# Free heads' output rows behind the second layer's first scores, and a shorter wait for runs of slots

## The chip, the cores and the metric

The kernel runs on one core of a Trainium2 chip. The metric is device time in microseconds (us); the time before is the median of three runs. One execution was also taken with the hardware profiler, and all rows below come from it. PE is the matmul engine, DVE and ACT are the vector and scalar engines, POOL the general one, and SP is the queue from which nearly all loads are issued.

## The reference

Eight batch rows, one token each, go twice through the same block A and block B, with the same weights and the same caches both times.

```python
def _A_ref(x, k_cache, v_cache, wq, wo):          # caches (8, 8, 4096, 256)
    q = (x @ wq).reshape(B, Sq, Hq, Dh)           # 16 query heads, 8 KV heads
    ...
    scores = jnp.einsum("bhqd,bhkd->bhqk", q, k) * (Dh ** -0.5)
    p = _softmax(scores, axis=-1)
    o = jnp.einsum("bhqk,bhkd->bhqd", p, v)
    return o...reshape(B, Sq, Hq * Dh) @ wo       # the output projection
...
x = x + _A_ref(_layernorm(x), A_k_cache, A_v_cache, A_wq, A_wo)
x = x + _B_ref(_layernorm(x), B_w1, B_w2, B_w3, B_w4)     # an MLP
x = x + _A_ref(...)      # second layer: same K and V, new queries
x = x + _B_ref(...)
```

A batch row's second-layer queries need the row's whole first layer and its MLP, but the K and V that they meet are those of the first layer. With one token, block B's shifts along the sequence fill all four parts with zeros, so that w1 and w2 have no effect; what stays is the layer norms and gelu(layernorm @ w3) @ w4, here called the MLP.

## The kernel before, in words

**Slots.** K and V stream through 30 slots of 512 KB (`QUARTERS`); a head's K or V is four slots, and a load takes up to four slots that lie side by side. In layer 0, five of a row's eight heads (3 to 7, "kept heads") leave their K in the slots, wholly or in part, and two leave V, so that the second layer need not load it again. Heads 0 to 2 are the "free heads": they keep nothing.

**The order of the work.** While a row goes from layer 0 to layer 1 (the "crossing": `mid`, a chain of small steps, the MLP and the new queries), the next row's free heads have their V products done: `run([("b", 0, b + 1, h) for h in free_heads])`. Their scores came earlier, and their V is loaded slot by slot (`MOST = 1`). Behind the crossing the row's second layer begins (`both(1, b, order2)`): its first heads' K stands in slots already, so their scores (line 1136) need only the new query, and they are what frees these slots.

**The planner.** `Plan.schedule` runs when the kernel is built. It is a list scheduler: every step (`plan.op`) has an engine, modelled durations, dependences and a priority, the lower the sooner. Whenever an engine is free in the model, it takes the ready step of lowest priority value. Program order is the usual priority (`len(plan.ops)`); short chains behind scores get `hi`, 100,000 lower, and the MLP's chain and the free heads' V products lower values still. The result is a fixed order of instructions on each engine, with semaphores where a step needs another engine's. When PE would idle, the planner puts in filler matmuls (line 1689).

**Output rows.** `wo_row` (line 1312, in `back`) multiplies one head's result `oT` with its part of `wo` in four matmuls and adds it up in one PSUM bank, `psR`, over the first seven heads of a row. `oT` has two buffers, so a head's `oT` (written on DVE, line 1292) waits for the row step of the head before the last. The bank is also used by the crossing's statistics (line 763), and the free heads' rows stand behind them in the program.

**Loads.** SP issues loads in one fixed order. For each, `next_kv` looks for a run of `m` free slots; it may wait for one until `late`, and then takes the largest run there is, so that the load goes out in pieces:

```python
late = max(free["sp"], dma_end - self.LEAD)
...
for t in [max(free["sp"], times[0])] + [x for x in times if free["sp"] < x <= late]:
    fit = [(k, a) for k, a in runs(t) if k >= m]
    if fit: break
else:
    t = max(late, times[0])
    m = min(m, max(k for k, a in runs(t)))
```

`dma_end` is when the planner thinks that the loads issued so far will have landed. It also thinks that a load starts 4.0 us (`ISSUE`) after its issue.

Of the kernel before, what the change touches and what calls it, by code (L numbers as in the profile page):

```python
# [52 lines left out]
Q1 = 176  # L53
ROWS = True
SHORT = 0.1


class Op:
# [28 lines left out]
class Plan:  # L87
# [5 lines left out]
    HOT = 3500  # L93


    ISSUE, LEAD = 4.0, 3.5
    BLOCK, FETCH = 128, 6.0
    LAT = {"pe": 0.25, "dve": 0.06, "act": 0.06, "pool": 0.05, "sp": 0.4}

# [374 lines left out]
def bass_interleave_layers__gqa_block_cached__mixer_s_mlp__decode_kernel(  # L474
# [20 lines left out]
    plan = Plan()  # L495
# [141 lines left out]
    def issue_kv(o, n, q):  # L637
# [6 lines left out]
        o.dma = (slot_sem[q], 16 * slot_n[q])  # L644
        o.dur = ((n << 15) / 26.88e3 + 8 * 0.008) / FASTER + SHORT * (n < 3)

# [55 lines left out]
    for i in range(2):  # L702
        plan.op("dve", lambda v, i=i: v.memset(psP[i][:, 0:DH], 0.0), 0.3, "const", wr=["pz"],
                banks=[f"P{i}"])
# [531 lines left out]
    def back(layer, b, h):  # L1236
# [10 lines left out]
        hi = len(plan.ops) - 10 ** 5  # L1247
# [6 lines left out]
        for u in range(4):  # L1254
# [17 lines left out]
            if u not in keep_v:  # L1272
# [7 lines left out]
                banks=[bk], prio=hi)  # L1280

        def sum_mm(t):
# [8 lines left out]
           prio=hi)  # L1291
# [14 lines left out]
        if k <= turn_at:  # L1306
            def wo_row(t):
                last = None
                for i in range(4):
                    a = (4 * h + i) * D  # L1310
                    r = 64 * layer + 32 * (i % 2)
                    last = t.matmul(psR[r:r + 1, 0:D], oT[no][:, i % 2, i // 2:i // 2 + 1],  # L1312
                                    wo_sb[:, a:a + D], start=(k == 1 and i < 2),
                                    stop=(k == turn_at and i >= 2),
                                    skip_group_check=True, tile_position=(0, r))
                return last
            o = plan.op("pe", wo_row, (0.41, 0.78, 448, 4), "wor", rd=[("oT", no), "wo0"], wr=[kr],
                        banks=["R"], prio=hi)
            if k == HOTK and layer == 0:
                o.hot = True  # L1320
        xkeys = [ok] + (["x3all" if b < B - 2 else ("xf", b - B + 2)] if layer else [])
        if k == turn_at:
            for a, mts in [(0, range(2)), (2 * P, range(2, NC5))]:
# [7 lines left out]
                def turn(t, a=a, mts=mts):  # L1331
# [7 lines left out]
                   prio=hi, width=YW)  # L1339
# [246 lines left out]
    free_heads = list(range(HKV - KEEP_K))  # L1586
# [19 lines left out]
    def run(tasks):  # L1606
        for t in tasks:
            (fronts_of if t[0] == "f" else back)(*t[1:])
# [140 lines left out]
```

## Time and profile before

| | |
|---|---|
| median of three runs | 1085.01 us (1085.01 to 1085.93) |
| profiled execution, its own time | 1082.09 us |
| its span, first to last instruction | 1080.2 us |
| loads in it | 436.38 MB, mean 404 GB/s |
| PE busy | 943.6 us (87%) |
| DVE, ACT busy | 598.8 us, 339.3 us |
| output rows (line 1312) | 444 matmuls, 65.1 us |
| loads of four slots, of one slot | 73 + 64, 130 + 11 |

In rows that group instructions stand line, engine, operation, output and inputs, shapes, count, busy time, the mean in ns, and the idle time before. In rows of a timeline the first two numbers are start and length in us. In rows of windows the pairs are an engine's busy time and its instructions, and the last three numbers are the granted PE clock, the share of the 16 DMA engines that was busy, and GB/s. In rows of waits stand the total, the number of waits and the longest one.

### The profile page before, as it was taken

The page shows a single profiled execution, that of the slowest core. Times are in us where ns is not written, and L with a number is a line of the kernel's source. Part 1 is how long each engine was busy: PE and PEld are TensorE (multiplying, and loading weights), DVE is VectorE, ACT ScalarE, POOL GpSimd, SP SyncE. Part 2 cuts the span into 40 slices and gives each one's busy share as a digit, 9 for nine tenths or more (in the row PEclk, how much of TensorE's full clock was granted, in tenths as well). Part 3 has the DMA queues.
Part 4 walks back from the last instruction along what each step waited for, and adds up shares of the span by engine and source line. Part 5 has one row for each costly group of instructions (what it writes and reads, how often), then busy time and mean ns, then how long its engine had stood idle before and what let it go on. Part 6 is the DMA issues. An engine that isn't in the chain of part 4 may idle for free.

```text
span 1080.2 us, 33935 instructions
## 1 busy us (share of the span) xinstructions
PE 943.6 (87%) x15144; PEld 651.1 (60%) x15144; DVE 598.8 (55%) x1895; ACT 339.3 (31%) x940; POOL 97.9 (9%) x278
## 2 busy tenths in 40 slices
PE   5889798988988889898898989998889999998895
PEld 4556556665656656566566655666556675666663
DVE  3345445555665556455565555565556655565564
ACT  1235113341234403254023531334214341343150
POOL 0000000000110101011010100101001000110010
PEclk9899989998999989999899998999989997999895
DMA  9999999999999999999999999999999999999994
GB/s 356 407 428 420 392 380 424 426 397 410 388 425 425 421 404 413 424 427 418 385 409 427 423 415 388 427 425 423 402 389 426 426 407 398 399 427 418 348 422 189
DMA packets 51342, 436.38 MB, mean 404 GB/s; under 512 B 5486, under 2 KB 8700, under 8 KB 27260
## 3 DMA queue, kind: packets, MB, share of 16 engines
q1 hardware_dynamic: 51108, 433.95, 97.9%
q8 instruction: 119, 1.95, 0.7%
q10 hardware_dynamic: 88, 0.26, 0.1%
q14 instruction: 27, 0.22, 0.1%
HBM read 434.18 MB, written 0.01 MB: 402 GB/s over the span
## 4 chain that ended last, share of the span: by engine, by line
DMA 50%; PE 39%; DVE 5%; issue 2%; SPq 1%; ACT 1%; POOL 0%; POOLq 0%; DVEq 0%
DMA kv<-in_A_k_cache_dram 27%; DMA kv<-in_A_v_cache_dram 22%; PE psT L1482 14%; PE psP L1262 7%; PE psT L1378 6%; PE psM L1136 3%; PE psM L891 2%; PE psR L1312 2%; PE psM L1053 1%; SPq L626 1%; DMA w_sb<-in_B_w_dram 1%; DVE kv L1413 1%; DVE oS L1276 1%; DVE oS L1278 1%; PE psP L1286 1%
## 5 line engine op out<-in xcount | busy, mean ns | idle before, releaser
L1482 PE MATMUL psT<-ident_f,kv 128*128 128x128 f32 x2752 | 376.3, 285 | 21.6 <-DMA kv<-in_A_k_cache_dram 19.3
L1482 PEld LDWEIGHTS psT<-ident_f,kv 128*128 128x128 f32 x2752 | 305.7, 144 | 101.2 <-issue 55.2
L1413 DVE COPY kv<-psT 128x512 f32<-128x512 f32 x381 | 260.8, 690 | 180.9 <-PE psT L1482 173.3
L1414 ACT COPY kv<-psT 128x512 f32<-128x512 f32 x339 | 197.5, 586 | 389.4 <-PE psT L1482 301.1
L1262 PE MATMUL psP<-kv,pT 128*2 128x256 bf16 x4096 | 178.3, 289 | 17.9 <-DMA kv<-in_A_v_cache_dram 14.5
L1378 PE MATMUL psT<-kv,qz 128*32 128x512 bf16 x1664 | 135.9, 399 | 6.3 <-ACT kv L1414 4.0
L1262 PEld LDWEIGHTS psP<-kv,pT 128*2 128x2 bf16 x4096 | 85.0, 83 | 62.1 <-DMA kv<-in_A_v_cache_dram 27.1
L1216 POOL PARTITION_ALL_REDUCE gm<-pm x128 | 45.4, 354 | 763.1 <-DVE pm L1214 754.2
L1276 DVE CAST oS<-psP 128x256 bf16<-128x256 f32 x128 | 53.9, 421 | 65.2 <-PE psP L1262 64.5
L1226 ACT ACTIVATE pT<-sS,nb,fac 128x32 bf16<-128x32 bf16 x128 | 52.6, 417 | 115.3 <-DVE nb L1220 115.3
L1312 PE MATMUL psR<-wo_sb,oT 128*1 128x448 bf16 x444 | 65.1, 377 | 9.9 <-DVE oT L1292 3.8
L1230 POOL PARTITION_ALL_REDUCE Db<-rs x128 | 51.0, 398 | 185.7 <-ACT pT L1226 185.7
L1286 PEld LDWEIGHTS psP<-sel,oS 128*128 128x128 bf16 x512 | 23.7, 99 | 61.4 <-DVE oS L1278 57.2
L1286 PE MATMUL psP<-sel,oS 128*128 128x2 bf16 x512 | 32.1, 166 | 31.9 <-DVE oS L1278 30.3
L1378 PEld LDWEIGHTS psT<-kv,qz 128*32 128x32 bf16 x1664 | 35.3, 96 | 40.3 <-issue 12.4
L1226 ACT ACTIVATE pT<-sS,nb 128x32 bf16<-128x32 bf16 x128 | 40.8, 326 | 59.2 <-DVE nb L1220 59.2
L1689 PE MATMUL psP<-ident_f 128*128 128x256 bf16 x357 | 58.2, 286 | 0.0
L1278 DVE TENSOR_TENSOR oS<-psP,oS 128x256 bf16<-128x256 f32 x128 | 54.1, 423 | 2.9
L1393 DVE CAST sr<-psT 128x512 bf16<-128x512 f32 x51 | 35.2, 691 | 31.9 <-PE psT L1378 31.7
L1136 PEld LDWEIGHTS psM<-qz,kv 128*128 128x128 bf16 x1344 | 41.2, 99 | 18.8 <-issue 5.8
L1136 PE MATMUL psM<-qz,kv 128*128 128x48 bf16 x1344 | 47.8, 187 | 5.4 <-DVE kv L1413 3.4
L1394 ACT CAST sr<-psT 128x512 bf16<-128x512 f32 x53 | 31.0, 585 | 53.4 <-PE psT L1378 53.4
(190 smaller groups left out, 778.8 us busy)
## 6 DMA issues: line engine op xcount, KB each, us to landing
kv<-in_A_k_cache_dram SPq DMA_DIRECT2D x73, 2048.0 KB, 22.2
kv<-in_A_v_cache_dram SPq DMA_DIRECT2D x64, 2048.0 KB, 19.0
kv<-in_A_v_cache_dram SPq DMA_DIRECT2D x130, 512.0 KB, 8.5
kv<-in_A_v_cache_dram SPq DMA_DIRECT2D x14, 1536.0 KB, 9.0
kv<-in_A_k_cache_dram SPq DMA_DIRECT2D x11, 1536.0 KB, 17.3
kv<-in_A_v_cache_dram SPq DMA_DIRECT2D x14, 1024.0 KB, 7.2
kv<-in_A_k_cache_dram SPq DMA_DIRECT2D x8, 1024.0 KB, 8.0
kv<-in_A_k_cache_dram SPq DMA_DIRECT2D x11, 512.0 KB, 14.1
```

Of the source, the lines that this page charges most:

```text
L1136: last = t.matmul(ps[:, SB + 2 * i:SB + 2 * i + 2 * REP], a()[:, c:256:2], bcast(rhs(c), REP, 1), start=(c == 0), stop=(c == 1))
L1226: return a.activation(pT[nr][:, :, :].rearrange("p i j -> p j i")[:, jj, :], sview[:, jj, :], ACT.Exp, bias=nb[nm][:, jj:jj + 1], scale=sc ...
L1262: last = t.matmul(ps[g4:g4 + 2, PV0:PV0 + DH], pT[nr][:, k, :], slot_ap(q, s * 256, 256), start=(i < 4), stop=(i >= 28), skip_group_check= ...
L1276: plan.op("dve", lambda v: v.tensor_copy(oS[:, 0, :], po), 0.36, "o", rd=[("pv", par, x) for x in range(4)], wr=["oS0"], banks=[bk], prio=hi)
L1278: plan.op("dve", lambda v: v.tensor_tensor(oS[:, 1, :], po, oS[:, 0, :], ALU.subtract), 0.36, "o", rd=["oS0"] + [("pv", par, x) for x in r ...
L1286: last = t.matmul(ps[:, PV1 + 2 * c:PV1 + 2 * c + 2], oS[:, w, c:DH:2], sel[:, :], start=(w == 0), stop=(w == 1))
L1312: last = t.matmul(psR[r:r + 1, 0:D], oT[no][:, i % 2, i // 2:i // 2 + 1], wo_sb[:, a:a + D], start=(k == 1 and i < 2), stop=(k == turn_at ...
L1378: last = t.matmul(psT[bank][32 * g:32 * g + 32, :], qz[:, a:a + 32], slot_ap(qs[g // 2], g % 2 * 1024, 1024)[:, c:1024:2], start=(half == ...
L1413: return e.tensor_copy(dst, psT[bank][:, :])
L1414: return e.copy(dst, psT[bank][:, :])
L1482: last = t.transpose(psT[bank][:, s * P:(s + 1) * P], src, ident_f[:, :])
L1689: return t.matmul(dst, ident_b, bcast(ident_b[:, 0:n // 4], 4, 1), start=True, stop=True)
```

## The change

Two edits. The row steps of layer 0's free heads, from batch row 1 on, get the priority of a step 100 places further on in the program, instead of one that is 100,000 places ahead. And the planner stops waiting for a run of slots 5.0 us before the end of its loads, instead of 3.5. Nothing that is computed changes.

```diff
 SHORT = 0.1
+WOR_AFTER = 100
...
-    ISSUE, LEAD = 4.0, 3.5
+    ISSUE, LEAD = 4.0, 5.0
...
             o = plan.op("pe", wo_row, (0.41, 0.78, 448, 4), "wor", rd=[("oT", no), "wo0"], wr=[kr],
-                        banks=["R"], prio=hi)
+                        banks=["R"], prio=len(plan.ops) + WOR_AFTER if layer == 0 and b and h in free_heads else hi)
```

## The prediction

> **What bounds the kernel now.** I read the page first, for the span, the engines, the DMA rate in 40 slices and the chain that ended last.
>
> ```profile
> span 1080.2 us, 33935 instructions
> ...
> GB/s 356 407 428 420 392 380 424 426 397 410 388 425 425 421 404 413 424 427 418 385 409 427 423 415 388 427 425 423 402 389 426 426 407 398 399 427 418 348 422 189
> DMA packets 51342, 436.38 MB, mean 404 GB/s; under 512 B 5486, under 2 KB 8700, under 8 KB 27260
> ...
> DMA 50%; PE 39%; DVE 5%; issue 2%; SPq 1%; ACT 1%; POOL 0%; POOLq 0%; DVEq 0%
> ```
>
> Half of the last chain is loads, and the bytes are fixed: at the 424 to 427 GB/s of the good slices 436.38 MB would take 436.38/425 = 1027 us. The row of 40 slices (27 us each) shows where the rest goes: besides the start and the end, one or two slices dip to 380 to 415 in each stretch of some five, once per batch row. So the second view is the table by windows at those dips; behind the length stand the busy times of PE, weight loads, DVE, ACT and POOL with their counts, then the granted clock, the DMA share and GB/s. First three dips, then a stretch of single-slot loads, then one of full loads:
>
> ```profile
> 270.00:280.00 10.00, 9.91 (x227) 6.33 (x224) 5.84 (x25) 1.06 (x4) 0.35 (x1) 0.76 0.96 325
> 400.00:410.00 10.00, 9.11 (x189) 5.76 (x189) 5.56 (x25) 2.40 (x7) 0.75 (x2) 0.77 1.00 381
> 1000.00:1030.00 30.00, 27.02 (x628) 19.84 (x621) 17.87 (x84) 5.79 (x16) 1.86 (x5) 0.86 0.97 353
> 390.00:400.00 10.00, 8.77 (x226) 5.79 (x223) 5.12 (x30) 0.21 (x1) 0.00 (x0) 0.88 1.03 407
> 430.00:440.00 10.00, 8.65 (x124) 5.95 (x120) 5.06 (x14) 4.26 (x12) 0.94 (x3) 1.00 1.00 424
> ```
>
> The dips are the crossings, where a batch row goes from layer 0 through the MLP to its second-layer queries. Two things are told apart by the last two rows: small loads alone cost a little (407 against 424), and something else in the crossing takes the rate down to 325 to 381. What the loads wait for there is in the waits of the SP queue, which issues them:
>
> ```profile
> SPq L643 <- PE psP L1262: 631.4, 137, 25.6
> ...
> SPq L643 <- PE psM L1136: 69.5, 30, 7.8
> ```
>
> A load waits until its slots are free, and slots are freed by PE: by the PV products (L1262) and by scores (L1136 is the form that the first heads after a crossing use). Elsewhere these waits are harmless because loads stand far ahead; in a crossing they decide. One crossing in the order of time, PE's own lines:
>
> ```profile
> 401.30 0.96 PE L1312 MATMUL psR<-wo_sb,oT 128*1 128x448 bf16 x4
> ...
> 402.47 0.95 PE L1312 MATMUL psR<-wo_sb,oT 128*1 128x448 bf16 x4
> 403.36 0.82 PE L1136 MATMUL psM<-qz,kv 128*128 128x48 bf16 x16
> ...
> 404.61 1.38 PE L1136 MATMUL psM<-qz,kv 128*128 128x48 bf16 x48
> ...
> 406.82 0.54 PE L1312 MATMUL psR<-wo_sb,oT 128*1 128x448 bf16 x4
> 407.30 0.40 PE L1689 MATMUL psP<-ident_f 128*128 128x256 bf16 x2
> ...
> 408.14 0.84 PE L1689 MATMUL psT<-ident_f 128*128 128x512 bf16 x3
> 409.62 0.37 PE L1136 MATMUL psM<-qz,kh 128*128 128x48 bf16 x8 [0.64 <-ACT kh L1422]
> ```
>
> and, from the same stretch, the query's last step on DVE, the oT of the third free head, and the load on SP:
>
> ```profile
> 401.15 0.21 DVE L1533 SCALAR_TENSOR_TENSOR qz<-cs_q,mom,psM 128x4 bf16<-128x4 f32 x1
> ...
> 406.17 0.15 DVE L1292 TENSOR_TENSOR oT<-psP,rc 128x4 bf16<-128x4 f32 x1
> ```
>
> ```profile
> 405.62 0.81 SPq L643 DMA_DIRECT2D kv<-in_A_v_cache_dram  x2
> ```
>
> The query is there at 401.15 + 0.21 = 401.36, but two output rows (L1312) of the next batch row's free heads run first, and the scores that free three slots start at 403.36 and end at 405.99; SP issues at 405.62, on their release. Behind the scores PE is short of work: it runs filler matmuls (L1689), 0.40 and 0.84, and idles 0.64.
>
> **Part one: 21 output rows move behind the scores.** They are layer 0, batch rows 1 to 7, heads 0 to 2: 84 of the matmuls of this group of the page.
>
> ```profile
> L1312 PE MATMUL psR<-wo_sb,oT 128*1 128x448 bf16 x444 | 65.1, 377 | 9.9 <-DVE oT L1292 3.8
> ```
>
> At four matmuls a step that is 21 of 111 steps. All seven crossings by window, L1312 alone, each from about the query to the end of the first head's scores (length, L1312 busy, clock, DMA share, GB/s; five of the rows and the sum):
>
> ```profile
> 139.40:143.60 4.20, 0.91 (x4) 0.73 0.94 338
> 273.10:277.70 4.60, 1.55 (x8) 0.81 1.05 304
> ...
> 528.60:534.60 6.00, 1.91 (x8) 0.53 1.00 382
> 658.20:663.10 4.90, 1.50 (x8) 0.76 0.97 340
> ...
> 915.70:921.20 5.50, 1.91 (x8) 0.62 1.02 381
> sum 34.90, PE 11.54; mean PE 1.65
> ```
>
> So 1.65 us of rows stand in front of the end of the scores in a crossing, 11.54 in all, mostly at half the clock (0.95 for four, against 0.54 at 406.82). With the new priority (program place plus 100, where it had been minus 100,000) they lose against everything that is ready within some two heads of program behind them, so the scores end up to 1.65 us sooner and so does the issue on them. The PV products keep their place, as they are more urgent in both. The rows themselves I cost at nothing: the two that join the third behind the scores take 2 x 0.54 = 1.08 us, under the 0.40 + 0.84 + 0.64 = 1.88 us of filler and idle there. If that cover is gone they cost 1.08 us in front of the second head's scores, and what the first scores gain the second lose. A row issues no DMA and stands in no queue but PE's. What waits for it: the DVE write of the third head's oT, which reuses the first head's buffer, behind it the PV bank of that head; and much later the seventh head's copies of the row sums.
>
> What 1.65 us sooner is worth is bounded by what DMA loses there. Against the 407 of single-slot loads, a window loses length x (407 - rate)/407: 4.20 x 69/407 = 0.71 in the first, 1.16 in the second, 0.35 in the last, and 4.26 us in all seven. Behind the scores the loss goes on, while the loads that the same chain releases come late; the windows there, with the filler (L1689) as the selected line (the first, the fifth and the last of seven):
>
> ```profile
> 143.60:152.00 8.40, 1.63 (x6) 1.00 0.94 346
> ...
> 663.10:670.00 6.90, 1.34 (x6) 1.00 1.01 421
> ...
> 921.20:928.00 6.80, 1.06 (x4) 1.00 1.00 379
> ```
>
> In the same way these lose 1.26 in the first, -0.24 in the fifth, 0.47 in the last and 3.74 in all seven. The filler in them (1.63, 1.34, 1.06; the others lie between) bears out that PE has room there in every crossing. The best is then -(4.26 + 3.74) = -8.0 us. The other end is a loss: one row at 0.54 in front of something needed, in seven crossings, +3.8. I take 3.0 of the 4.26, because a loss of 0.61 in the mean is smaller than the 1.65 by which the release comes forward, but some of it lies ahead of the release and belongs to PV; and 1.0 of the 3.74, which only inherits the shift: **-4.0 us**.
>
> **Part two: LEAD from 3.5 to 5.0.** When the slots for a load of m are not free together, the planner waits for them until 3.5 us before it thinks the queue will run dry, then sends a smaller piece. Now it stops 1.5 us sooner. The order of loads on SP is the same; pieces become smaller and leave earlier. Where loads stand far ahead the limit is not reached, so this too acts in the crossings, and alone in the last one, which has no rows to move: there 30 x (407 - 353)/407 = 4.0 us are lost, the most that it could return beside part one. Its price is more small loads. At 407 GB/s a slot of 512 KB (524,288 B) takes 1.288 us and at 424 it takes 1.237, so a slot cut off costs 0.052 us. Today's pieces:
>
> ```profile
> kv<-in_A_k_cache_dram SPq DMA_DIRECT2D x73, 2048.0 KB, 22.2
> kv<-in_A_v_cache_dram SPq DMA_DIRECT2D x64, 2048.0 KB, 19.0
> kv<-in_A_v_cache_dram SPq DMA_DIRECT2D x130, 512.0 KB, 8.5
> ```
>
> Most of the 130 are cut on purpose (84 belong to the seven rows' free heads, loaded slot by slot). If 30 slots more are cut, the price is 30 x 0.052 = 1.6 us; if none, nothing. For the gain I take 1.6, some 40% of the last crossing's 4.0. Gain and price cancel: **0**, between -4.0 and the +9.4 of the second rival.
>
> **The sum** is made against the profiled execution's 1082.09 us (span 1080.2 and 1.9 around it), which is 2.9 below the median of the runs, 1085.01: 1082.1 - 4.0 = 1078.1 there, and 1085.0 - 4.0 = **1081.0 us** as a median.
>
> **Rivals.** *Nothing to win (1085).* The dips may not be late releases. For it: the DMA share at 400 to 410 is 1.00 at 381 GB/s, so the engines are counted as busy, with longer packets, not as empty. Against: the lowest rates of the crossings (304, 338, 340) stand in the windows with the rows in front. It gives within 2.2 us of no change.
>
> *Small loads (1090).* A planner that gives up sooner leaves slots scattered, and then later runs of four are missing too, in the good stretches also. 137 loads have four slots; if a third of them, 45, break into singles, that is 180 x 0.052 = 9.4 us, less the 4.0: 1085.0 + 5.4 = 1090.4. The turning point is 77 more slots loaded singly (4.0/0.052). For it: pieces are already common in crossings. Against: the two rows of four-slot loads land 19 to 22 us after issue, about four loads ahead at 2 MB / 424 GB/s = 4.9 us each, where the new limit is not reached. At the far end, if each cut-off slot came to an empty queue and cost its own 1.29 us once more, 30 of them would cost 39 us and the time would be 1120; of the 0.22 below I give this 0.02.
>
> The Trainium skill, "DMA: Bandwidth & Descriptors", section Measured, speaks against this part: it asks for transfers of at least 1 MiB, and its section on the anatomy of one DMA puts a fixed 2.0 us on each, measured on GpSimd's path. By that, 30 further loads would cost an estimated 60 us if nothing hid it. The trace does not bear it out for loads in a queue, as the loads of 388 to 404 show, an answer of the DMA view:
>
> ```profile
> DMA packets 1682, 6.44 MB, mean 402 GB/s; under 512 B 187, under 2 KB 187, under 8 KB 1610
> ...
> kv<-in_A_v_cache_dram SPq DMA_DIRECT2D x9, 512.0 KB, 7.3
> kv<-in_A_v_cache_dram SPq DMA_DIRECT2D x1, 1024.0 KB, 7.6
> ```
>
> Nine loads of one slot and one of two, issued in 16 us, go with a mean of 402 GB/s, 1.3 us a slot; the rule has 2.0 + 1.2.
>
> *The rows come too late (1089).* If the planner puts the first head's row behind the second head's scores, past 412, the third head's oT waits some 6 us (it is written at 406.17 now), its PV bank is held, and the slots of the next head on that bank come free late. If 0.54 us per crossing is lost, it is the +3.8 above: 1085.0 + 3.8 = 1088.8. Against: the filler at 407 to 409 shows free PE before that.
>
> **How the numbers follow.** 2.2 us (0.2%) is about what a measurement of this kernel can tell from no change. Forecast 0.50; nothing to win 0.20; small loads 0.22; rows too late 0.08. So faster 0.50, same 0.20, slower 0.30. The range reaches from the best of part one with the forecast's gain of part two unpaid (1085.0 - 8.0 - 1.6 = 1075.4, rounded to 1075.5) to the small loads' 1090. What is left out is the far end of the small loads and the case that all of the crossings' loss comes back with the last one's. The forecast's own range is 1076 to 1082.5.
>
> **What would show it.** Right: in the crossings L1136 comes straight behind the query's qz, with no L1312 between them; L1312 stands where L1689 stood, with fewer fillers; SP's wait on L1136 is shorter than 69.5; the seven windows' rates rise from 304 to 382 GB/s towards 407, with the slices' dips. For part two: more than 130 loads of 512 KB, by up to some 30, and the window 1000 to 1030 above 353. Wrong: rates in the crossings as before although L1136 is earlier (the first rival); over 77 more single-slot loads or good slices under 420 (the second); a new wait of DVE at L1292 for L1312 (the third).

## The result, and the profile after

| | before | after |
|---|---|---|
| median of the runs, us | 1085.47 | 1078.49 |
| ratio to before, 95% interval | | 0.9931 [0.9911, 0.9950] |
| the same, runs repeated later on one chip | 1086.97 | 1079.43, 0.9941 [0.9917, 0.9964] |
| profiled execution, its span, us | 1080.2 | 1074.4 |

The change makes the kernel 0.6 to 0.7% faster. The forecast was 4 us, the median moved by 7. The two halves of the forecast were wrong in opposite directions, as the experiments show: the moved rows give nothing, and the shorter wait, priced at nothing, gives all of it. That the time still fell into the forecast's range is luck: one error made up for part of the other. Single executions scatter (those of the kernel before from 1079 to 1093 us over all its runs), so ratios of many runs decide below and profiles tell only where.

The page after, and the waits of SP (lines stand one further down than before, from 56 on):

```profile
span 1074.4 us, 33999 instructions
...
GB/s 367 407 426 422 391 390 427 426 419 399 408 426 425 416 394 420 425 426 409 382 423 425 425 414 397 426 425 423 399 397 423 427 415 398 409 426 417 355 423 193
DMA packets 56526, 436.39 MB, mean 406 GB/s; under 512 B 6062, under 2 KB 9276, under 8 KB 34236
...
DMA 49%; PE 42%; DVE 4%; SPq 2%; issue 1%; ACT 1%; POOL 0%; DVEq 0%
```

```profile
SPq L644 <- PE psP L1263: 530.7, 139, 27.1
SPq L644 <- PE psT L1379: 195.6, 48, 18.0
SPq L644 <- PE psM L1137: 65.9, 36, 5.1
```

SP waits 100 us less for the PV products (631.4 before) and 90 more for the scores in rows (L1379, 106.6 before): the waits have changed places and not gone. The waits for the first heads' scores, which the moved rows were to shorten, are nearly as before (69.5). The good slices are as before (423 to 427), so the further small loads have not spread into them. The pieces:

```profile
kv<-in_A_k_cache_dram SPq DMA_DIRECT2D x68, 2048.0 KB, 23.2
kv<-in_A_v_cache_dram SPq DMA_DIRECT2D x61, 2048.0 KB, 17.1
kv<-in_A_v_cache_dram SPq DMA_DIRECT2D x163, 512.0 KB, 8.1
...
kv<-in_A_k_cache_dram SPq DMA_DIRECT2D x28, 512.0 KB, 9.5
```

There are 191 one-slot loads where there were 141, and 129 of four slots where there were 137. The crossings, first from the query to the end of the first head's scores with the output rows (L1313) selected, then behind it with the filler (L1690), in windows that follow the shifted times:

```profile
137.20:143.10 5.90, 0.91 (x4) 0.50 1.00 376
268.90:274.50 5.60, 0.91 (x4) 0.57 0.98 374
...
911.30:916.30 5.00, 0.00 (x2) 0.58 1.00 372
sum 35.20, PE 4.73; mean PE 0.68
```

```profile
143.10:151.50 8.40, 1.69 (x6) 0.94 0.99 353
...
659.90:666.80 6.90, 0.84 (x3) 1.00 1.02 411
...
916.30:923.10 6.80, 1.12 (x4) 1.00 1.02 405
```

Of the 11.54 us of rows in front of the scores' end 4.73 are left, but the seven windows up to it are no shorter: 35.2 us against 34.9. The loss of both sets of windows against 407 GB/s has fallen from 8.0 to 3.2 us. That isn't the whole account: in the ten us ahead of each query the rates are lower than before (372 in the mean, against 396), which gives 4.0 us back. The windows alone do not say where the time went. One crossing on PE, at the same place as in the prediction:

```profile
397.72 0.96 PE L1313 MATMUL psR<-wo_sb,oT 128*1 128x448 bf16 x4
...
399.33 1.23 PE L1137 MATMUL psM<-qz,kv 128*128 128x48 bf16 x32
...
400.81 0.57 PE L1137 MATMUL psM<-qz,kv 128*128 128x48 bf16 x16
401.67 0.39 PE L1263 MATMUL psP<-kv,pT 128*2 128x256 bf16 x8 [0.29 <-DMA kv<-in_A_v_cache_dram]
402.00 0.57 PE L1137 MATMUL psM<-qz,kv 128*128 128x48 bf16 x16
402.50 0.54 PE L1313 MATMUL psR<-wo_sb,oT 128*1 128x448 bf16 x4
```

One row still comes first; the second has moved behind the scores. In its stead PE waits 0.29 us, in the middle of the scores, for a V load of the free heads.

### The profile page after: what moved, and what is told of

Same layout as the page of the kernel before. It is cut to its first block, busy times and chain, and to the rows that moved or that the text cites. A ratio compares the mean times of both kernels' runs of the same rounds, so it can differ in the third digit from the quotient of the medians.

```text
span 1074.4 us, 33999 instructions
## 1 busy us (share of the span) xinstructions
PE 943.5 (88%) x15150; PEld 651.8 (61%) x15150; DVE 593.6 (55%) x1889; ACT 344.1 (32%) x946; POOL 97.9 (9%) x278
## 4 chain that ended last, share of the span: by engine, by line
DMA 49%; PE 42%; DVE 4%; SPq 2%; issue 1%; ACT 1%; POOL 0%; DVEq 0%
DMA kv<-in_A_k_cache_dram 30%; DMA kv<-in_A_v_cache_dram 18%; PE psT L1483 16%; PE psP L1263 8%; PE psT L1379 5%; PE psM L1137 3%; PE psR L1313 2%; SPq L627 2%; PE psM L892 1%; PE psM L1054 1%; PE psP L1690 1%; DVE kv L1414 1%; DMA w_sb<-in_B_w_dram 1%; DVE oS L1279 1%; DVE oS L1277 1%
## 5 line engine op out<-in xcount | busy, mean ns | idle before, releaser
L1414 DVE COPY kv<-psT 128x512 f32<-128x512 f32 x368 | 252.9, 691 | 189.2 <-PE psT L1483 180.1
L1415 ACT COPY kv<-psT 128x512 f32<-128x512 f32 x352 | 205.3, 587 | 384.7 <-PE psT L1483 300.6
L1379 PE MATMUL psT<-kv,qz 128*32 128x512 bf16 x1664 | 133.7, 395 | 4.7 <-ACT kv L1415 3.4
L1313 PE MATMUL psR<-wo_sb,oT 128*1 128x448 bf16 x444 | 62.4, 366 | 8.2 <-DVE oT L1293 4.0
L1379 PEld LDWEIGHTS psT<-kv,qz 128*32 128x32 bf16 x1664 | 34.6, 95 | 38.1 <-issue 12.3
L1690 PE MATMUL psP<-ident_f 128*128 128x256 bf16 x359 | 56.7, 284 | 0.0
L1394 DVE CAST sr<-psT 128x512 bf16<-128x512 f32 x55 | 38.0, 692 | 31.2 <-PE psT L1379 31.0
L1137 PEld LDWEIGHTS psM<-qz,kv 128*128 128x128 bf16 x1344 | 43.6, 102 | 18.0 <-issue 8.1
L1137 PE MATMUL psM<-qz,kv 128*128 128x48 bf16 x1344 | 50.5, 191 | 4.1 <-issue 2.2
L1395 ACT CAST sr<-psT 128x512 bf16<-128x512 f32 x49 | 28.7, 586 | 52.1 <-PE psT L1379 49.5
## 6 DMA issues: line engine op xcount, KB each, us to landing
kv<-in_A_v_cache_dram SPq DMA_DIRECT2D x7, 1536.0 KB, 11.1
```

Source lines behind the costliest of these rows:

```text
L1137: last = t.matmul(ps[:, SB + 2 * i:SB + 2 * i + 2 * REP], a()[:, c:256:2], bcast(rhs(c), REP, 1), start=(c == 0), stop=(c == 1))
L1379: last = t.matmul(psT[bank][32 * g:32 * g + 32, :], qz[:, a:a + 32], slot_ap(qs[g // 2], g % 2 * 1024, 1024)[:, c:1024:2], start=(half == ...
L1414: return e.tensor_copy(dst, psT[bank][:, :])
L1415: return e.copy(dst, psT[bank][:, :])
L1690: return t.matmul(dst, ident_b, bcast(ident_b[:, 0:n // 4], 4, 1), start=True, stop=True)
```

## The experiments

**The two halves alone, and the change again.** Theory A is the prediction's (the rows carry it), theory B that the shorter wait does, C that each needs the other. Rows alone, from the changed kernel:

```diff
-    ISSUE, LEAD = 4.0, 5.0
+    ISSUE, LEAD = 4.0, 3.5
```

> The rows alone: WOR_AFTER as in the change, LEAD back at 3.5. Theory A (the prediction's): the rows carry the gain; about 4 us faster than before, a ratio of 0.996, and one-slot loads stay near before's 130 + 11. Theory B: the shorter wait carries the gain, since in the changed kernel one row per crossing still runs before the first scores and the first head's scores end no sooner on the mean; then within 2 us of before, 0.998 to 1.002. Theory C: the two need each other; then this one is slower than before.

Measured: 1.0029 [1.0009, 1.0049], slower. The wait alone, from the kernel before:

```diff
-    ISSUE, LEAD = 4.0, 3.5
+    ISSUE, LEAD = 4.0, 5.0
```

> The shorter wait alone: LEAD 5.0, the output rows as before. Theory A: within 1.5 us of before (gain and price of smaller loads cancel), 0.9985 to 1.0015. Theory B: all or most of the gain, 4 to 7 us faster, 0.9935 to 0.996, with some 50 more one-slot loads, as in the changed kernel. Theory C: slower than before or no change.

Measured: 0.9940 [0.9920, 0.9959]. The change once more:

> The changed kernel itself once more, beside the two halves on the same chip. All theories: 0.991 to 0.995, as first measured. It gives the sum against which the halves are added, and a second profile: where its lead over before in loaded bytes comes at the same places as in the first, it belongs to the schedule; where it does not (one step of 1.6 us at 100 MB, away from a crossing), it belongs to the single execution.

Measured: 0.9941 [0.9917, 0.9964]. So B holds: the wait alone gives as much as both. A falls, and so does C, which had both halves slower or useless alone. The step at 100 MB that this expectation names is in the second profile too (between 90 and 100 loaded MB the lead over before's trace grows by 1.4 us, by 1.6 in the first). So by the expectation's own rule it belongs to the schedule, but not all of it: the traces with LEAD at 3.5 gain 0.6 to 0.7 us on before's there as well.

**The rows' place, with everything else held.** The rows alone also got another plan, so two kernels keep the plan of before. In the first, 13 rows are put behind the scores in PE's finished order (`line`; `j` is the place behind the last of these scores):

```diff
     plan.schedule()
+    for o in reversed([o for o in line if o in moved_rows]):
...
+        line.insert(j, o)
     plan.synchronise()
```

> The kernel before with its plan kept to the last slot, load and priority; in PE's finished order alone the 13 free-head rows that stood in front of the first head's scores are put straight behind them. Theory A (the prediction's step: sooner scores are sooner loads): 3 to 4 us faster, 0.996 to 0.997. Theory B (the scores' end is not what the loads in the crossing are short of, and the rows only change places): within 1 us of before, 0.999 to 1.001. Theory C (the third head's oT and with it slots come late): 2 us slower or more. If this one is not slower, then what made the rows alone slower (1.0029) was the planner's other slots and loads, not the rows' place.

Measured: 1.0016 [0.9998, 1.0033]. In the second, the rows compute one of their 448 columns and leave out the others, so that their time is all but gone:

```diff
-  last = t.matmul(psR[r:r + 1, 0:D], ..., wo_sb[:, a:a + D], ...)
+  w = 1 if layer == 0 and b and h in free_heads else D
+  last = t.matmul(psR[r:r + 1, 0:w], ..., wo_sb[:, a:a + w], ...)
```

> The kernel before with its plan kept; the 21 free-head row steps compute one of their 448 columns (the other columns of these heads are left out of the projection), so nearly all of their PE time is gone from the crossings: up to 11.5 us of it in front of the first scores' end. It is the most that moving them could ever give. Theory A (scores in time are loads in time): 4 us faster or more, 0.996 or less. Theory B (the rows' place does not matter to the loads): within 1.5 us of before, 0.9985 to 1.0015.

Measured: 0.9993 [0.9972, 1.0013]. So theory A falls here too: both intervals lie above its 0.996 to 0.997, and hold theory B's no change. Even taking nearly all of the rows' time away is worth nothing that can be measured. The first kernel's timeline shows why; this is the same crossing as in the prediction:

```profile
403.27 0.59 PE L1265 MATMUL psP<-kv,pT 128*2 128x256 bf16 x8 [0.28 <-DMA kv<-in_A_v_cache_dram]
403.79 0.82 PE L1137 MATMUL psM<-qz,kv 128*128 128x48 bf16 x16
404.54 0.60 PE L1265 MATMUL psP<-kv,pT 128*2 128x256 bf16 x8
405.07 2.10 PE L1137 MATMUL psM<-qz,kv 128*128 128x48 bf16 x48
407.10 1.47 PE L1315 MATMUL psR<-wo_sb,oT 128*1 128x448 bf16 x8
```

The last 48 of the scores as a window, first before, then in this kernel (length, L1136 or L1137 busy, clock, DMA share, GB/s):

```profile
404.61:405.99 1.38, 1.38 (x48) 1.00 0.99 365
```

```profile
405.07:407.17 2.10, 2.10 (x48) 0.50 1.00 361
```

No row stands before the scores, but PV products do, and they wait for their V to land; and the last 48 score matmuls take 2.10 us where they took 1.38. Over the seven crossings, from the query's row sums, the first score starts at 2.07 us (2.08 with the thin rows) instead of 2.58, and the first head's scores end at 5.66 (5.73) instead of 5.60. So of the 1.65 us of rows only 0.5 come out as an earlier start (in this crossing PV products and a wait for V stand in front of the scores), and the scores then take those 0.5 us back, since they run at a lower clock. From the first score to the last the granted clock is 0.80 in the mean of before's seven crossings, 0.55 with the rows moved by hand and 0.52 with the thin ones, and the 64 matmuls are busy for 2.31, 2.89 and 2.97 us. Why the clock is lower there no run shows.

**What a small load costs.**

```diff
...
-  o.emit = lambda eng: eng.dma_start(dst, src)
...
+  for i in range(n):
+      d = eng.dma_start(kv[:, (q + i) * 2048:(q + i + 1) * 2048], src[:, i * 2048:(i + 1) * 2048])
...
```

> The kernel before with its plan kept; every load of 2, 3 or 4 slots is issued as that many loads of one slot at the same moment, one behind the other. It prices small loads alone, without any earlier issue. Prediction's price: 0.052 us for a slot loaded singly; 137 x 4 + 25 x 3 + 22 x 2 = 667 slots, so 35 us slower, 1.032. By the packets' own times (159 against 614/4 = 153.5 ns for 4 KB) 667 x 8 x 5.5 ns = 29 us, 1.027. If a load had a fixed price that the queue does not hide, much more: at 1 us each over 480 further loads 480 us. If small pieces help by themselves, as each can be worked on when it lands, less than 20 us.

Measured: 1127.39 us against 1087.39, 1.0369 [1.0344, 1.0393]. 40.0 us over 667 slots are 0.060 us a slot; the prediction had 0.052.

```profile
GB/s 339 399 408 406 381 371 409 407 392 404 361 408 408 404 374 398 408 409 406 376 406 407 409 406 378 407 407 408 377 372 408 408 387 383 384 408 388 293 402 195
...
kv<-in_A_v_cache_dram SPq DMA_DIRECT2D x456, 512.0 KB, 11.4
```

The price is a lower rate everywhere, 408 in slices that had 425. A fixed price for each load can't be large: the 483 further loads cost 0.083 us each, all told.

**How long the planner should wait.** From 3.5 in both directions, with the rows as before except in the second:

> LEAD 4.25, rows as before: half of the step from 3.5 to 5.0. If what pays is that loads leave sooner (loads issued under 4 us before the one ahead of them lands: 19 in before, 4 at LEAD 5.0), about half of the gain: 2 to 4 us faster than before, 0.996 to 0.998, with one-slot loads between 141 and 203. If the gain at 5.0 is a lucky plan (another draw of slots), no order in LEAD: anywhere from 0.993 to 1.003.

Measured at 4.25: 0.9932 [0.9908, 0.9956], all of the gain and not half.

> LEAD 6.5 with the rows moved as in the change: the same step of 1.5 again. Theory A: slower than the changed kernel by the price of further pieces, 0.052 us for each slot loaded singly (30 more: 1.6 us). Theory B: if earlier issue is what pays and the rate in the crossings (352 to 410 GB/s in the five us behind the query) has room left up to 407, a further 1 to 3 us faster; if the queue stands far enough ahead at 5.0, no change or slower by the pieces.

Measured at 6.5, rows moved: 0.9950 [0.9932, 0.9968], no further gain.

> LEAD 8.0, rows as before: the planner hardly waits for runs. The late loads are gone as at 5.0, and the price of small loads goes on: some 100 one-slot loads more than before at 0.052 us are 5 us, and fewer four-slot loads. If early issue and price are the two terms: the gain of 5.0 kept and another 2 to 5 us of price, so 0.996 to 0.999. If small loads cost nothing: as at 5.0, 0.994.

Measured at 8.0: 0.9958 [0.9939, 0.9977]; 246 one-slot loads.

> LEAD 2.0, rows as before: the planner waits 1.5 us longer for runs than before. If late loads are the cost (20 issued under 4 us before the one ahead lands, which lose 11.9 us in before's trace; 6 and 4.4 us at 4.25), more of them and later ones: 5 to 20 us slower than before, 1.005 to 1.02, although it has fewer one-slot loads. If the price of small loads were what decides, faster than before.

Measured at 2.0: 1.0123 [1.0090, 1.0156], although it has the fewest one-slot loads, 126. All four plans above 3.5 are faster and the one below it is slower, so the gain isn't one lucky plan. What too long a wait does is plainest in this kernel, on SP and in windows of 1 us (POOL's busy time, the clock, the DMA share, GB/s):

```profile
542.06 1.17 SPq L643 DMA_DIRECT2D kv<-in_A_v_cache_dram  x2
```

```profile
541.00:542.00 1.00, 0.00 (x0) 1.00 0.21 74
542.00:543.00 1.00, 0.35 (x1) 1.00 0.00 0
543.00:544.00 1.00, 0.03 (x1) 1.00 1.07 188
544.00:545.00 1.00, 0.36 (x1) 1.00 0.89 319
545.00:546.00 1.00, 0.12 (x1) 1.00 1.00 426
```

```profile
SPq L643 <- PE psP L1262: 6.3, 2, 5.6
```

```profile
kv<-in_A_v_cache_dram SPq DMA_DIRECT2D x1, 1024.0 KB, 5.0
```

SP waited up to 5.6 us for PV products to free a run of two slots; the queue ran empty; and the load, issued at 542.06, moved nothing before 543 and landed after 5.0 us, where its 1 MB takes 2.5 at 424 GB/s. So this load, which came to an empty queue, lost some 2.5 us. The Trainium skill, "DMA: Bandwidth & Descriptors", section on the anatomy of one DMA, has about 2.0 us of fixed cost for a DMA that GpSimd issues; these loads are issued by SP.

Counted over whole traces, a load is called late here if it is issued less than 4 us before the load ahead of it lands; it loses what its landing lies behind that one beyond 1.228 us a slot (1.272 for a single slot), which is what most loads take that are issued well ahead. Two loads in the first 3 us of the kernel, which no LEAD touches, are left out; the expectation for LEAD 2.0 counts them, and so has 20 and 11.9 us for before, and 6 and 4.4 for 4.25.

| kernel | LEAD | ratio | late loads, us lost | one-slot loads |
|---|---|---|---|---|
| wait 2.0 | 2.0 | 1.0123 | 20, 20.6 | 126 |
| before | 3.5 | 1 | 18, 9.8 | 141 |
| rows alone | 3.5 | 1.0029 | 17, 14.2 | 145 |
| rows by hand | 3.5 | 1.0016 | 15, 13.3 | 141 |
| thin rows | 3.5 | 0.9993 | 14, 14.7 | 141 |
| wait 4.25 | 4.25 | 0.9932 | 4, 1.5 | 173 |
| wait 5.0 | 5.0 | 0.9940 | 3, 3.6 | 203 |
| the change | 5.0 | 0.9931 | 5, 4.5 | 191 |
| the change again | 5.0 | 0.9941 | 4, 2.1 | 191 |
| wait 6.5, rows moved | 6.5 | 0.9950 | 1, 0.0 | 225 |
| wait 8.0 | 8.0 | 0.9958 | 2, 1.5 | 246 |

From 3.5 to 4.25 the late loads go, and beyond it their number hardly falls any more while the price goes on: 8.0 is 0.26% (2.8 us) behind 4.25 with 73 more one-slot loads, which at 0.060 would be 4.4; the two intervals overlap.

Single traces scatter too much to be compared one by one: that of the wait alone has a longer span (1082.4 us) than before's (1080.2). In the mean of the four at 3.5 and of seven above it (the last run below is the seventh) the account closes. Late loads lose 13.0 and 1.9 us, so 11.1 less; all other loads lose much the same, 24.3 and 25.3; and 59 more one-slot loads at 1.272 - 1.228 = 0.044 us cost 2.6. That leaves 7.4 us, and the mean spans differ by 6.9 (1085.6 and 1078.7).

The loss is no step at 4 us. Over these traces and the two below, loads issued less than 2 us before the one ahead lands lose 2.2 us in the mean (8 loads), from 2 to 3 us 1.2 (30), from 3 to 4 us 0.6 (72), from 4 to 4.5 us 0.3 (109), and beyond 5 us 0.1 or less.

**Is it the latency, or the planner's own reckoning?** 3.5 lies under the planner's `ISSUE` of 4.0, so it let itself wait until after the point from which it foresees a gap.

```diff
-    ISSUE, LEAD = 4.0, 3.5
+    ISSUE, LEAD = 3.0, 3.5
```

> ISSUE 3.0 with LEAD 3.5, rows as before: LEAD is now above the latency that the planner reckons with, but it still waits for runs until 3.5 us before its queue ends. Theory B1 (a load that in truth leaves under 4 us ahead loses time): little changes, at most 2 us faster than before, 0.998 to 1.0, with late loads about as many as before. Theory B2 (what hurt was the relation: a wait allowed to the point at which the planner itself foresees a gap, LEAD below ISSUE): most of the gain, 0.993 to 0.996.

Measured: 0.9949 [0.9928, 0.9969], with 6 late loads (5.7 us) and 163 one-slot loads. That is what B2 expected in time; but the late loads have fallen too, against B1's assumption, so the run does not tell the two apart. In either case there are fewer loads that come late.

**The best of both.** The changed kernel with LEAD 4.25 in place of 5.0:

> LEAD 4.25 with the rows moved: the candidate for the best. The shorter wait was worth 0.9932 at 4.25 without the rows, and the rows alone 1.0029. If the rows are worth nothing, 0.992 to 0.9945, as the changed kernel; if they cost what they cost alone, 0.995 to 0.997.

Measured: 0.9930 [0.9906, 0.9955], 1079.66 us, with one late load (0.3 us) and 176 one-slot loads. It can't be told from the change (0.9931, 0.9941) or from 4.25 without the rows (0.9932). None of the versions beats the change beyond its interval. Again the rows, this time with a LEAD that is large enough, change nothing.

## Why the prediction was right or wrong

*What bounds the kernel* was right: loads, and their dips in the crossings. Part of that loss is late loads, which the values of LEAD turn off and on.

*Part one, -4.0 us, was wrong: it measured nothing.* The step that failed is "so the scores end up to 1.65 us sooner and so does the issue on them". The rows' 1.65 us were taken as time that everything behind them would gain. The first score starts 0.5 us sooner, and the scores end where they ended (5.66 and 5.73 us against 5.60): PV products that wait for their own loads stand in front of them and among them, and the scores run at a granted clock of 0.5 instead of 0.8, which the prediction's sum has no term for. The range of this part (from -8.0 to +3.8) held the result. That the rows cost nothing behind the scores is possible, but the rows alone were 0.3% slower. Two rows of before's timeline that the prediction left out could have warned, PV products among the scores of the same crossing:

```profile
401.92 0.76 PE L1262 MATMUL psP<-kv,pT 128*2 128x256 bf16 x8
...
404.11 0.57 PE L1262 MATMUL psP<-kv,pT 128*2 128x256 bf16 x8
```

*Part two, 0, was mis-sized: it measured about 0.6%, 6.5 us.* The mechanism was right (pieces smaller, sooner; acting in the crossings). The terms were not, and nor was the bound: 6.5 is beyond the -4.0 that the prediction called the most. The term that failed is the gain of 1.6, taken from the last crossing alone because the first seven had been given to part one. Before's trace has 3.2 us of late loads in the last crossing, but 6.1 more in four of the first seven (the first, second, fourth and seventh), and the other traces at 3.5 have more still in all. The price was 1.6 for 30 slots; the change has 50 one-slot loads more and the wait alone 62, at the measured 0.060 3.0 and 3.7 us. What could have warned is that 3.5 is less than the 4.0 that stands in front of it on the same line.

*The rivals.* Nothing to win: no, though it holds for the rows. Small loads: the price was right in kind and nearly in size (0.060 for 0.052), but the runs of slots did not fall apart; four-slot loads went from 137 to 129, and the good slices stayed at 425. At LEAD 8.0 there are 108 loads of four slots, and it still is faster than before. Rows too late: DVE's one long wait for L1313 was there before and did not grow (5.1 us before, 4.1 after). A loss of some 2 us a load, as under the rule that the prediction cites, was regular only where the queue was about to run dry (the 8 loads above); five of these 8 stand in the trace at LEAD 2.0, and none in those at 4.25 and above.

*The signs.* More one-slot loads came (50, not 30), and SP's wait for scores is shorter (65.9), but by too little to mean anything. The window from 1000 to 1030 went from 353 to 380 GB/s (364 for 996 to 1026), as forecast. The rates of the seven windows rose in four, fell in two and stayed in one. Of "no L1312 between the query and L1136" half came true, and with no effect. The sign of fewer fillers came true behind the scores (7.58 us against 9.05), but not over the whole kernel (359 against 357 of the commoner form). Of the signs of being wrong none came.

## What to carry to other kernels

Before a step is moved out of the way, look at what stands next to it and at the clock: if what stands there waits for data, or then runs at a lower clock, moving the step may gain nothing. A kernel with the step thinned out tells it in one run. Where a planner keeps a queue full, compare what it waits for with what it risks: here a load issued less than 2 us before the queue ran dry lost about 2.2 us, and a smaller load cost 0.06 us a slot. Change the two halves of an edit one at a time: here one gave everything and the other nothing.

## What was not expected of the hardware, and what stays open

A load issued to an empty queue showed no bytes for about 1 us (issued at 542.06, the first at 543.02) and landed some 2.5 us later than its size asks for; behind other loads the same size lands in 1.2 to 1.3 us a slot. Loads of one slot run at 408 GB/s where those of four run at 425. With work taken away in front of them, the scores ran at a granted clock of 0.5 where it had been 0.8.

Open: why the rows alone were slower (1.0029). By hand they were 1.0016 with an interval that reaches 0.9998, so the planner's other slots may be the cause, or the rows' place may cost a little; the runs don't separate the two. Whether latency or the planner's foreseen gap sets the point between 3.5 and 4.25. And why the clock is lower where the rows are gone.
